# A fused short convolution and leaky-ReLU MLP on one Trainium2 core: the taps' load and softmax, the weight loads and the warm-up matmuls are rearranged

## The chip, the core and the metric

The kernel runs on one core of a Trainium2 chip. A core has five engines with an instruction queue each: TensorE (PE in the profile, its weight loads PEld), VectorE (DVE), ScalarE (ACT), GpSimd (POOL) and SyncE (SP). Data moves between the chip's main memory and the on-chip memory by DMA; a load or store is asked for by an instruction in the queue of SP, ACT or POOL. Engines wait for each other, and for DMAs, by semaphores. The metric is the time of the program on the device in microseconds (us).

## What is computed

The input `x` is 8 x 4096 x 192 (batch, sequence, channels), in float32. The channels form 8 heads of 24; each head has 7 taps.

```python
w = softmax(weight, axis=-1)                  # (8 heads, 7 taps)
# causal convolution along the sequence, the same taps for all 24 channels of a head
out[b, s, h, g] = sum_k w[h, k] * x_pad[b, s + k, h, g]     # 6 zeros ahead of the sequence
h = out.reshape(32768, 192) @ moe_w_in         # (192, 2048)
g = np.maximum(0.01 * h, h)
result = g @ moe_w_out                         # (2048, 192), float32
```

## The kernel before

The 32768 tokens are cut into 32 blocks: a block is 512 positions of two batch rows at a time (index `e`, 0 or 1). Channels are cut into 3 chunks (`c`) of 64, so that 64 channels of row `e = 0` lie on partitions 0 to 63 and the same channels of row `e = 1` on partitions 64 to 127. The stages of a block:

- `load_x` (line 71): two DMAs from SP, one for each `e`, into `x_nat`, float32, tokens on partitions, 384 KB each. Three buffers.
- `cast_x` (line 83): to bfloat16, `x_bf`. In the loop on ScalarE, in halves; for block 0 one half on VectorE and one on ScalarE.
- `transpose_x` (line 96): 24 small matmuls with the identity on TensorE, to PSUM tiles `ptr`; `evac_x` (line 112) copies them to `xt`, channels on partitions.
- `conv_jobs` (lines 128 and 134): for each chunk seven VectorE operations, one multiply and six multiply-adds, with the taps `wk[:, c, k]` as a scalar for each partition. The result is `yt`.
- `mm1` (lines 235 and 242): for each of 16 slices `f` of 128 of the 2048 inner features, six matmuls of 64 rows (three chunks, two `e`, which use the two halves of the array) to the PSUM tile `ph`, and a ScalarE activation (Prelu, alpha 0.01) to `g`.
- `mm2` (line 253): the second product, 128 tokens at a time into `po`, with `w_out` as the moving operand; `evac_o` (line 295) copies `po` to `o_sb` on VectorE, and SP stores it (line 298).

The loop over blocks runs the first product of block `blk` beside the second product of block `blk - 1`; the convolution of block `blk + 1`, and the cast and transposes of block `blk + 2`, are spread over the eight steps of a block. So in the first pass of the loop there is no second product, and `w_out` is used from the second pass on. The order of the instructions on each engine is the order in which the code is written (`manual_schedule`); the tile framework puts in the waits. It hands the DMAs of SP and ACT eight completion semaphores in turn (`DMAHW0` to `DMAHW7` in the rows below), and a DMA that takes one again waits first for the DMA that had it.

Ahead of the loop stands the start, on which the change works. Before: SP loads block 0 of x; the raw taps are loaded straight into `wk`, spread over the partitions by 14 small DMAs with a repeated source, dealt in turn to ACT, POOL and SP (line 163); SP loads block 1, then `moe_w_in` into the float32 tile `w_stage` in eight DMAs (line 172: four quarters of the features, each twice, once for each half of the partitions); POOL loads `w_out` with a cast to bfloat16 (line 177); SP loads block 2. Then block 0 is cast, transposed and copied, the softmax of the taps is done on 128 partitions (lines 192 to 202), block 0 is convolved, block 1 is cast, transposed and copied, and ScalarE casts the four quarters of `w_stage` to `w_in` (line 215). TensorE then runs 56 warm-up matmuls into a tile that nobody reads (line 221), of which each uses 64 rows of the array. They stand in TensorE's queue ahead of the first product.

Of the kernel before, what the change touches and what calls it, by code (L numbers as in the profile page):

```python
# [9 lines left out]
FP32 = mybir.dt.float32  # L10
BF16 = mybir.dt.bfloat16
# [3 lines left out]
def kernel(  # L15
# [8 lines left out]
    nc = tc.nc  # L24

    B, S, D = x.shape
    H, K = weight.shape
    Din, F = moe_w_in.shape
    GRP = D // H
    HALO = 16  # L30
# [4 lines left out]
    CH = 64  # L35
    NCH = D // CH
    ST = 512
    SUB = ST // 128
    NFC = F // 128
# [6 lines left out]
    WQ = 4  # L46

    const_pool = ctx.enter_context(tc.tile_pool(name="const", bufs=1))
# [4 lines left out]
    g_pool = ctx.enter_context(tc.tile_pool(name="g", bufs=3))  # L53
    o_pool = ctx.enter_context(tc.tile_pool(name="o", bufs=4))
    psum_h = ctx.enter_context(tc.tile_pool(name="ph", bufs=2, space=bass.MemoryType.PSUM))
# [7 lines left out]
    x_nat, x_bf, xt, ptr = {}, {}, {}, {}  # L63

    def load_x(blk):
        if blk >= NBLK:
            return
        rp, st = divmod(blk, NB)
        t = stage_pool.tile([128, 2, SUB, D], FP32, name="x_nat")
        for e in range(2):  # L70
            nc.sync.dma_start(  # L71
                out=t[:, e, :, :],
                in_=x[2 * rp + e, st * ST : (st + 1) * ST, :].rearrange(
                    "(c p) d -> p c d", p=128
                ),
            )
        x_nat[blk] = t

    def cast_x(blk, e, copy, half=None):
        if blk not in x_bf:  # L80
            x_bf[blk] = xb_pool.tile([128, SUB, NCH, 2, CH], BF16, name="x_bf")
        s = slice(0, SUB) if half is None else slice(half * SUB // 2, (half + 1) * SUB // 2)
        copy(  # L83
            out=x_bf[blk][:, s, :, e, :],
            in_=x_nat[blk][:, e, s, :].rearrange("p s (c k) -> p s c k", c=NCH),
        )
# [16 lines left out]
    def evac_x(blk, copy):  # L103
        rp, st = divmod(blk, NB)
        if st == 0:
            xt[rp] = xt_pool.tile([128, NCH, HALO + S], BF16, name="xt")
            nc.vector.memset(xt[rp][:, :, 0:HALO], 0.0)
        dst = xt[rp][:, :, HALO + st * ST : HALO + (st + 1) * ST].rearrange(
            "p c (s i k) -> p i s c k", s=SUB, i=2
        )  # L110
        for i, t in enumerate(ptr.pop(blk)):
            copy(out=dst[:, i], in_=t)  # L112
# [4 lines left out]
    def conv_jobs(blk):  # L117
        rp, st = divmod(blk, NB)
        y = yt_pool.tile([128, NCH, ST], BF16, name="yt")
        yt[blk] = y  # L120
        jobs = []
        for c in range(NCH):
            for k in range(K):
                src = xt[rp][:, c, BASE + k + st * ST : BASE + k + (st + 1) * ST]
                dst = y[:, c, :]
                if k == 0:
                    jobs.append(
                        lambda s=src, d=dst, c=c: nc.vector.tensor_scalar_mul(  # L128
                            d, s, wk[:, c, 0:1]
                        )  # L130
                    )
                else:
                    jobs.append(
                        lambda s=src, d=dst, c=c, k=k: nc.vector.scalar_tensor_tensor(  # L134
                            out=d, in0=s, scalar=wk[:, c, k : k + 1], in1=d,
                            op0=mybir.AluOpType.mult, op1=mybir.AluOpType.add,
                        )
                    )
        return jobs


    load_x(0)
    ident = const_pool.tile([128, 128], BF16)
    make_identity(nc, ident)

    wk = const_pool.tile([128, NCH, K], FP32, name="wk")
    parts = []
    for c in range(NCH):
        lo = c * CH
        while lo < (c + 1) * CH:  # L150
            h = lo // GRP
            n = 1
            hi = min((h + 1) * GRP, (c + 1) * CH)
            if lo == h * GRP:
                while (h + n + 1) * GRP <= (c + 1) * CH:
                    n += 1
                    hi = (h + n) * GRP
            parts += [(e * CH + lo - c * CH, c, h, n, (hi - lo) // n) for e in range(2)]
            lo = hi
    queues = [nc.scalar, nc.gpsimd, nc.sync]  # L160
    for i, (p, c, h, n, m) in enumerate(parts):
        src = weight[h : h + n, :]
        queues[i % 3].dma_start(  # L163
            out=wk[p : p + n * m, c, :],
            in_=bass.AP(tensor=src.tensor, offset=src.offset, ap=[[K, n], [0, m], [1, K]]),
        )
    load_x(1)
    w_stage = g_pool.tile([128, NCH, F], FP32, name="w_stage", tag="g")
    for q in range(WQ):
        for e in range(2):  # L170
            fs = slice(q * F // WQ, (q + 1) * F // WQ)
            nc.sync.dma_start(
                out=w_stage[e * CH : (e + 1) * CH, :, fs],
                in_=moe_w_in[:, fs].rearrange("(c p) f -> p c f", p=CH),
            )
    w_out = const_pool.tile([128, NFC, D], BF16)
    nc.gpsimd.dma_start(out=w_out, in_=moe_w_out.rearrange("(c p) d -> p c d", p=128))  # L177
    load_x(2)


    nmax = const_pool.tile([128, NCH], FP32)
    ssum = const_pool.tile([128, NCH], FP32)
    junk = const_pool.tile([128, 1], FP32)
    nc.vector.memset(junk, 0.0)
    nc.scalar.activation(out=junk, in_=junk, func=mybir.ActivationFunctionType.Exp)  # L185

    cast_x(0, 0, nc.vector.tensor_copy)
    cast_x(0, 1, nc.scalar.copy)
    transpose_x(0)
    evac_x(0, nc.vector.tensor_copy)  # L190

    nc.vector.tensor_reduce(  # L192
        out=nmax, in_=wk, axis=mybir.AxisListType.X, op=mybir.AluOpType.max,
    )
    nc.vector.tensor_sub(wk, wk, nmax.unsqueeze(2).to_broadcast((128, NCH, K)))  # L195
    nc.scalar.activation(out=wk, in_=wk, func=mybir.ActivationFunctionType.Exp)  # L196
    nc.vector.tensor_reduce(
        out=ssum, in_=wk, axis=mybir.AxisListType.X, op=mybir.AluOpType.add,
    )
    nc.vector.tensor_scalar_add(ssum, ssum, 1e-9)  # L200
    nc.vector.reciprocal(ssum, ssum)
    nc.vector.tensor_mul(wk, wk, ssum.unsqueeze(2).to_broadcast((128, NCH, K)))

    for job in conv_jobs(0):
        job()

    cast_x(1, 0, nc.scalar.copy)
    cast_x(1, 1, nc.scalar.copy)
# [4 lines left out]
    for q in range(WQ):  # L213
        fs = slice(q * F // WQ, (q + 1) * F // WQ)
        nc.scalar.copy(out=w_in[:, :, fs], in_=w_stage[:, :, fs])  # L215


    wa = psum_h.tile([128, 2, ST], FP32, name="warm", tag="ph")
    NWARM = 56
    for i in range(NWARM):  # L220
        nc.tensor.matmul(  # L221
            out=wa[:, 0, :], lhsT=ident[0:CH, :], rhs=xt[0][0:CH, 0, HALO : HALO + ST],
            start=(i == 0), stop=(i == NWARM - 1),
        )


    g, po, osb, seal = {}, {}, {}, {}
# [75 lines left out]
    for blk in range(NBLK + 1):  # L303
# [3 lines left out]
        for j in range(STEPS):  # L307
            n = (blk - 1) * STEPS + j
# [47 lines left out]
```

## Time and profile before

| | us |
|---|---|
| time, median of 3 runs | 740.72 (740.41 to 740.81) |
| time of the profiled execution | 740.75 |
| its span, first to last instruction | 738.9 |
| TensorE busy, of the span | 712.5 (96%) |
| VectorE busy | 567.0 (77%) |
| ScalarE busy | 555.1 (75%) |
| GpSimd busy | 5.0 (1%) |
| first block of x being cast on VectorE, start | 4.44 |
| first convolution, start | 15.69 |
| warm-up, start | 20.89 |
| first activation `g`, start | 46.29 |

Busy time is a share of the whole span; for a change at the start it tells little. What matters here are the times of single events in the first 70 us. In the profile's rows, L221 is line 221 of the kernel, an arrow `a<-b` means that the instruction writes tile a and reads b, x56 is the number of instructions, and in the timeline the square bracket behind a row tells how long the engine had been idle and who released it. A release is inferred: where an instruction waits for several things, the one that came last by the profile is named. Rows that begin with two numbers have the start and the duration, both in us. A suffix q (SPq, ACTq) means the engine's queue issuing a DMA.

### The profile page before, as it was taken

The page shows a single profiled execution, that of the slowest core. Times are in us where ns is not written, and L with a number is a line of the kernel's source. Part 1 is how long each engine was busy: PE and PEld are TensorE (multiplying, and loading weights), DVE is VectorE, ACT ScalarE, POOL GpSimd, SP SyncE. Part 2 cuts the span into 40 slices and gives each one's busy share as a digit, 9 for nine tenths or more (in the row PEclk, how much of TensorE's full clock was granted, in tenths as well). Part 3 has the DMA queues.
Part 4 walks back from the last instruction along what each step waited for, and adds up shares of the span by engine and source line. Part 5 has one row for each costly group of instructions (what it writes and reads, how often), then busy time and mean ns, then how long its engine had stood idle before and what let it go on. Part 6 is the DMA issues. An engine that isn't in the chain of part 4 may idle for free.

```text
span 738.9 us, 26161 instructions
## 1 busy us (share of the span) xinstructions
PE 712.5 (96%) x11944; PEld 608.2 (82%) x11944; DVE 567.0 (77%) x1002; ACT 555.1 (75%) x644; POOL 5.0 (1%) x12
## 2 busy tenths in 40 slices
PE   0998999999999999999999999999999999999998
PEld 0335788888888888888888888888888888888887
DVE  2944888888888888888888888888888888888812
ACT  1448778887777888877778887777888877778771
POOL 2000000000000000000000000000000000000000
PEclk9999999999999999999999999999999999999999
DMA  8900222122222212222222122222212222211111
GB/s 162 247 19 2 87 77 66 56 87 78 88 77 87 77 45 77 88 77 78 87 77 68 54 88 77 88 76 88 77 48 75 87 78 79 85 34 46 34 45 65
DMA packets 72901, 55.96 MB, mean 76 GB/s; under 512 B 5712, under 2 KB 71254, under 8 KB 72790
## 3 DMA queue, kind: packets, MB, share of 16 engines
q1 hardware_dynamic: 70368, 53.49, 23.9%
q0 software_dynamic: 2224, 0.80, 1.0%
q8 instruction: 93, 1.52, 0.8%
q14 instruction: 18, 0.15, 0.1%
q10 hardware_dynamic: 198, 0.00, 0.0%
HBM read 29.90 MB, written 25.17 MB: 75 GB/s over the span
## 4 chain that ended last, share of the span: by engine, by line
PE 95%; DMA 2%; ACT 2%; ACTq 0%; issue 0%; SPq 0%; DVE 0%
PE po L253 46%; PE ph L235 44%; PE warm L221 3%; ACT g L242 2%; DMA x_nat<-in_x_dram 2%; PE ptr L96 2%; DMA wk<-in_weight_dram 1%; ACT x_bf L83 0%; ACTq L163 0%; SPq L71 0%; SPq L163 0%; DVE o_sb L295 0%
## 5 line engine op out<-in xcount | busy, mean ns | idle before, releaser
L242 ACT ACTIVATE g<-ph 128x1024 bf16<-128x1024 f32 x512 | 496.4, 1021 | 144.1 <-PE ph L235 132.6
L134 DVE SCALAR_TENSOR_TENSOR yt<-xt,wk,yt 128x512 bf16<-128x512 bf16 x576 | 431.2, 749 | 14.0
L253 PEld LDWEIGHTS <-g 64*128 64x128 bf16 (+1 forms) x8048 | 374.9, 94 | 32.4 <-issue 0.2
L253 PE MATMUL po<-w_out,g 64*128 64x192 bf16 (+1 forms) x8048 | 399.2, 243 | 0.0
L235 PE MATMUL ph<-yt,w_in 64*128 64x512 bf16 x3072 | 395.1, 377 | 3.3 <-ACT g L242 2.7
L235 PEld LDWEIGHTS <-w_in 64*128 64x128 bf16 x3072 | 233.3, 94 | 59.6 <-issue 9.5
L295 DVE COPY o_sb<-po 128x192 f32<-128x192 f32 x256 | 91.4, 357 | 106.7 <-PE po L253 103.9
L83 ACT CAST x_bf<-x_nat 128x384 bf16<-128x384 f32 (+1 forms) x123 | 64.1, 521 | 3.7 <-DMA x_nat<-in_x_dram 3.7
L112 DVE COPY xt<-ptr 128x768 bf16<-128x768 bf16 x62 | 31.7, 552 | 37.8 <-PE ptr L96 37.8
L96 PE MATMUL ptr<-ident,x_bf 64*128 64x64 bf16 x768 | 19.2, 193 | 19.4 <-ACT x_bf L83 19.4
L96 PEld LDWEIGHTS <-x_bf 64*128 64x128 bf16 x768 | 17.6, 97 | 19.8 <-ACT x_bf L83 19.6
L128 DVE TENSOR_SCALAR yt<-xt,wk 128x512 bf16<-128x512 bf16 x96 | 33.2, 346 | 0.1
L221 PE MATMUL warm<-xt,ident 64*128 64x512 bf16 x56 | 24.1, 631 | 0.0
L221 PEld LDWEIGHTS <-ident 64*128 64x128 bf16 x56 | 8.2, 147 | 15.0 <-issue 15.0
L215 ACT CAST w_in<-w_stage 128x1536 bf16<-128x1536 f32 x4 | 5.9, 1472 | 6.3 <-DMA w_stage<-in_moe_w_in_dram 6.3
L196 ACT ACTIVATE wk<-wk 128x21 f32<-128x21 f32 x1 | 0.2, 222 | 7.6 <-DVE wk L195 7.6
L185 ACT ACT_TABLE_LOAD x1 | 1.3, 1283 | 4.7 <-issue 4.7
L192 DVE TENSOR_REDUCE nmax<-wk 128x3 f32<-128x21 f32 x1 | 0.2, 174 | 5.3 <-DMA x_nat<-in_x_dram 5.3
L83 DVE CAST x_bf<-x_nat 128x768 bf16<-128x768 f32 x1 | 0.7, 657 | 3.6 <-DMA x_nat<-in_x_dram 3.6
L163 POOL DMA_DIRECT2D wk<-in_weight_dram x5 | 3.1, 651 | 0.3 <-issue 0.3
L112 ACT COPY xt<-ptr 128x768 bf16<-128x768 bf16 x2 | 1.5, 802 | 0.9 <-PE ptr L96 0.9
L177 POOL DMA_DIRECT2D w_out<-in_moe_w_out_dram x1 | 1.2, 1248 | 0.0
(14 smaller groups left out, 2.3 us busy)
## 6 DMA issues: line engine op xcount, KB each, us to landing
x_nat<-in_x_dram SPq DMA_DIRECT2D x64, 384.0 KB, 4.4
out_dram<-o_sb SPq DMA_DIRECT2D x128, 192.0 KB, 1.9
w_stage<-in_moe_w_in_dram SPq DMA_DIRECT2D x8, 384.0 KB, 13.9
w_out<-in_moe_w_out_dram POOLq DMA_DIRECT2D x1, 768.0 KB, 12.6
wk<-in_weight_dram ACTq DMA_DIRECT2D x3, 1.3 KB
wk<-in_weight_dram POOLq DMA_DIRECT2D x3, 1.3 KB, 3.9
wk<-in_weight_dram SPq DMA_DIRECT2D x2, 0.4 KB, 5.8
wk<-in_weight_dram SPq DMA_DIRECT2D x2, 0.2 KB
```

The source lines that it names most:

```text
L83: copy(out=x_bf[blk][:, s, :, e, :], in_=x_nat[blk][:, e, s, :].rearrange("p s (c k) -> p s c k", c=NCH),)
L96: nc.tensor.transpose(out=ts[i][:, s, c, :], in_=x_bf[blk][ps, s, c, :, :].rearrange("p e k -> p (e k)"), identity=ident[ps, ps],)
L112: copy(out=dst[:, i], in_=t)
L128: lambda s=src, d=dst, c=c: nc.vector.tensor_scalar_mul(d, s, wk[:, c, 0:1])
L134: lambda s=src, d=dst, c=c, k=k: nc.vector.scalar_tensor_tensor(out=d, in0=s, scalar=wk[:, c, k : k + 1], in1=d, op0=mybir.AluOpType.mult, ...
L163: queues[i % 3].dma_start(out=wk[p : p + n * m, c, :], in_=bass.AP(tensor=src.tensor, offset=src.offset, ap=[[K, n], [0, m], [1, K]]),)
L215: nc.scalar.copy(out=w_in[:, :, fs], in_=w_stage[:, :, fs])
L221: nc.tensor.matmul(out=wa[:, 0, :], lhsT=ident[0:CH, :], rhs=xt[0][0:CH, 0, HALO : HALO + ST], start=(i == 0), stop=(i == NWARM - 1),)
L235: nc.tensor.matmul(out=ph[:, e, :], lhsT=w_in[ps, c, f * 128 : (f + 1) * 128], rhs=y[ps, c, :], start=(c == 0), stop=(c == NCH - 1),)
L242: return nc.scalar.activation(out=g[blk][:, f, :, :], in_=ph, func=mybir.ActivationFunctionType.Prelu, alpha=0.01,)
L253: ins = nc.tensor.matmul(out=po[m], lhsT=g[b][ps, fc, e, s * 128 : (s + 1) * 128], rhs=w_out[ps, fc, :], start=(rt != 1 and fc == 0), stop ...
L295: nc.vector.tensor_copy(out=o_sb[:, n % 2, :], in_=po.pop(n))
```

## The change

1. Taps. One DMA from ACT loads the 8 x 7 taps into `w8`, with heads on 8 partitions. The softmax runs on those 8 partitions. GpSimd builds a 0/1 mask `sel` (8 x 384) with a memset and two `affine_select`; three float32 matmuls with `sel` as the stationary operand copy each head's taps to the partitions of its channels, into a PSUM tile `wps`, from which VectorE copies them to `wk`. All of this stands ahead of block 0's cast in VectorE's and TensorE's queues.
2. x block 1 is asked for right after block 0, with no tap load between.
3. `w_in`: the DMAs for the lower half of the partitions stay on SP, those for the upper half go to ACT, written behind ACT's cast of block 0 and ahead of its casts of block 1. The convolution of block 0 now stands ahead of these loads in the code.
4. `w_out`: its load stays on POOL, now behind a copy of one element of `w_stage` (`pjunk`), the last element of the lower half's last quarter, so it is asked for once that DMA has landed.
5. Warm-up: 40 matmuls instead of 56, each over all 128 rows of the array instead of 64.

The diff, with the softmax and parts that only move left out:

```diff
     load_x(0)
+    w8 = const_pool.tile([H, K], FP32, name="w8")
+    nc.scalar.dma_start(out=w8, in_=weight)
+    load_x(1)
     ident = const_pool.tile([128, 128], BF16)
     make_identity(nc, ident)
+    sel = const_pool.tile([H, NCH, 2, CH], FP32, name="sel")
+    nc.gpsimd.memset(sel, 1.0)
+    for sign, off in ((1, 0), (-1, GRP - 1)):
+        nc.gpsimd.affine_select(
+            out=sel, in_=sel, compare_op=mybir.AluOpType.is_ge, fill=0.0,
+            base=off, channel_multiplier=-sign * GRP,
+            pattern=[[sign * CH, NCH], [0, 2], [sign, CH]],
+        )
...
+    wps = psum_h.tile([128, 2, ST], FP32, name="wps", tag="ph")
+    for c in range(NCH):
+        nc.tensor.matmul(
+            out=wps[:, 0, c * K : (c + 1) * K],
+            lhsT=sel[:, c, :, :].rearrange("h e k -> h (e k)"),
+            rhs=w8, start=True, stop=True,
+        )
...
-        queues[i % 3].dma_start(
-            out=wk[p : p + n * m, c, :],
-            in_=bass.AP(tensor=src.tensor, offset=src.offset, ap=[[K, n], [0, m], [1, K]]),
-        )
-    load_x(1)
...
-            nc.sync.dma_start(
+            (nc.sync, nc.scalar)[e].dma_start(
                 out=w_stage[e * CH : (e + 1) * CH, :, fs],
                 in_=moe_w_in[:, fs].rearrange("(c p) f -> p c f", p=CH),
             )
-    w_out = const_pool.tile([128, NFC, D], BF16)
-    nc.gpsimd.dma_start(out=w_out, in_=moe_w_out.rearrange("(c p) d -> p c d", p=128))
     load_x(2)
...
+    pjunk = const_pool.tile([1, 1], FP32)
+    nc.gpsimd.tensor_copy(out=pjunk, in_=w_stage[0:1, NCH - 1, F - 1 : F])
+    w_out = const_pool.tile([128, NFC, D], BF16)
+    nc.gpsimd.dma_start(out=w_out, in_=moe_w_out.rearrange("(c p) d -> p c d", p=128))
...
-    NWARM = 56
+    NWARM = 40
     for i in range(NWARM):
         nc.tensor.matmul(
-            out=wa[:, 0, :], lhsT=ident[0:CH, :], rhs=xt[0][0:CH, 0, HALO : HALO + ST],
+            out=wa[:, 0, :], lhsT=ident, rhs=xt[0][:, 0, HALO : HALO + ST],
             start=(i == 0), stop=(i == NWARM - 1),
         )
```

How the instructions stand on the engines. SyncE's queue from the second load of x on, before; each row is a DMA, and the square bracket the semaphores that the instruction waits for:

```order
L71 DMA x_nat<-in_x_dram 128x4x192 x2
L163 DMA wk<-in_weight_dram 16x1x7
L163 DMA wk<-in_weight_dram 8x1x7 [waits DMAHW0_49]
L163 DMA wk<-in_weight_dram 8x1x7 [waits DMAHW1_49]
L163 DMA wk<-in_weight_dram 16x1x7 [waits DMAHW2_49]
L71 DMA x_nat<-in_x_dram 128x4x192 [waits DMAHW3_49]
L71 DMA x_nat<-in_x_dram 128x4x192 [waits DMAHW4_49]
L172 DMA w_stage<-in_moe_w_in_dram 64x3x512 [waits DMAHW5_49]
L172 DMA w_stage<-in_moe_w_in_dram 64x3x512 [waits DMAHW6_49]
```

The same place after:

```order
L71 DMA x_nat<-in_x_dram 128x4x192 x4
L202 DMA w_stage<-in_moe_w_in_dram 64x3x512 x2
L202 DMA w_stage<-in_moe_w_in_dram 64x3x512 [waits DMAHW1_49]
L202 DMA w_stage<-in_moe_w_in_dram 64x3x512 [waits DMAHW3_49]
L71 DMA x_nat<-in_x_dram 128x4x192 [waits DMAHW5_49]
```

The four tap loads and their waits are gone from between blocks 0 and 1 of x, six loads go out without a wait, and four of the w_in loads have left this queue.

ScalarE's queue from the start, after (before, five tap loads stood first, and no w_in load was in it); `w_87` is the tile `w8`:

```order
L144 DMA w_87<-in_weight_dram 8x7
L160 ACT_TABLE_LOAD
L160 ACTIVATE junk<-junk 128x1 [waits DVE_49]
L169 ACTIVATE w_87<-w_87,nmax 8x7 [waits DMAHW0_49,DVE_49]
L83 CAST x_bf<-x_nat 128x12x64 [waits DMAHW2_49]
L202 DMA w_stage<-in_moe_w_in_dram 64x3x512 x3
L202 DMA w_stage<-in_moe_w_in_dram 64x3x512 [waits DMAHW4_49]
L83 CAST x_bf<-x_nat 128x12x64 [waits DMAHW3_49]
L83 CAST x_bf<-x_nat 128x12x64
```

The exponential of the softmax now stands ahead of block 0's cast, and four w_in loads stand ahead of block 1's casts, the last of them with a wait for the second half of block 1 of x (`DMAHW4`).

VectorE's queue from the start, before:

```order
L184 MEMSET junk 128x1
L83 CAST x_bf<-x_nat 128x12x64 [waits DMAHW1_49]
L107 MEMSET xt 128x3x8
L112 COPY xt<-ptr_132 128x4x3x64 [waits PE_49]
L112 COPY xt<-ptr_133 128x4x3x64 [waits PE_49]
L192 TENSOR_REDUCE nmax<-wk 128x3 [waits DMAHW1_49,DMAHW2_49,DMAHW0_49,DMAHW3_49,DMASW4_49,DMAHW5_49,DMASW3_49,DMAHW6_49,DMASW2_49,DMAHW7_49,DMASW1_49,DMASW0_49]
```

And after:

```order
L159 MEMSET junk 128x1
L165 TENSOR_REDUCE nmax<-w_87 8x1 [waits DMAHW0_49]
L172 TENSOR_REDUCE ssum<-w_87 8x1 [waits Activation_49]
L175 TENSOR_SCALAR ssum<-ssum 8x1 [waits DVE_49]
L176 RECIPROCAL ssum<-ssum 8x1 [waits DVE_49]
L177 TENSOR_SCALAR w_87<-w_87,ssum 8x7 [waits DVE_49]
L186 COPY wk<-wps 128x21 [waits PE_49]
L83 CAST x_bf<-x_nat 128x12x64 [waits DMAHW1_49]
L107 MEMSET xt 128x3x8
L112 COPY xt<-ptr_121 128x4x3x64 [waits PE_49]
```

The softmax has moved ahead of block 0's cast, and it waits for one load in place of twelve.

More of the change, by code (lines that the diff above doesn't have):

```diff
@@ L142 @@
     load_x(0)
+    w8 = const_pool.tile([H, K], FP32, name="w8")
+    nc.scalar.dma_start(out=w8, in_=weight)
+    load_x(1)
     ident = const_pool.tile([128, 128], BF16)
     make_identity(nc, ident)
-    wk = const_pool.tile([128, NCH, K], FP32, name="wk")
[L147 to L163, printed above, removed]
-            out=wk[p : p + n * m, c, :],
-            in_=bass.AP(tensor=src.tensor, offset=src.offset, ap=[[K, n], [0, m], [1, K]]),
-        )
-    load_x(1)
+    sel = const_pool.tile([H, NCH, 2, CH], FP32, name="sel")
[6 more added lines that the diff above has]
+        )
@@ new lines @@
+    junk = const_pool.tile([128, 1], FP32)
+    nc.vector.memset(junk, 0.0)
+    nc.scalar.activation(out=junk, in_=junk, func=mybir.ActivationFunctionType.Exp)
+    nmax = const_pool.tile([H, 1], FP32)
+    ssum = const_pool.tile([H, 1], FP32)
+    nc.vector.tensor_reduce(
+        out=nmax, in_=w8, axis=mybir.AxisListType.X,
+        op=mybir.AluOpType.max, negate=True,
+    )
+    nc.scalar.activation(
+        out=w8, in_=w8, func=mybir.ActivationFunctionType.Exp, bias=nmax, scale=1.0,
+    )
@@ new lines @@
+    nc.vector.tensor_reduce(
+        out=ssum, in_=w8, axis=mybir.AxisListType.X, op=mybir.AluOpType.add,
+    )
+    nc.vector.tensor_scalar_add(ssum, ssum, 1e-9)
+    nc.vector.reciprocal(ssum, ssum)
+    nc.vector.tensor_scalar_mul(w8, w8, ssum)
+    wps = psum_h.tile([128, 2, ST], FP32, name="wps", tag="ph")
[4 more added lines that the diff above has]
+            rhs=w8, start=True, stop=True,
+        )
@@ L168 @@
+    wk = const_pool.tile([128, NCH, K], FP32, name="wk")
+    nc.vector.tensor_copy(
+        out=wk, in_=wps[:, 0, 0 : NCH * K].rearrange("p (c k) -> p c k", c=NCH)
+    )
+    cast_x(0, 0, nc.vector.tensor_copy)
+    cast_x(0, 1, nc.scalar.copy)
+    transpose_x(0)
+    evac_x(0, nc.vector.tensor_copy)
+    for job in conv_jobs(0):
+        job()
     w_stage = g_pool.tile([128, NCH, F], FP32, name="w_stage", tag="g")
@@ L175 @@
             )
-    w_out = const_pool.tile([128, NFC, D], BF16)
-    nc.gpsimd.dma_start(out=w_out, in_=moe_w_out.rearrange("(c p) d -> p c d", p=128))
     load_x(2)
[L181 to L205, printed above, removed]
     cast_x(1, 0, nc.scalar.copy)
```

## The prediction

> **What bounds the kernel now.** I read the page first, then the chain of waits over the first 70 us, then the timeline of each engine over the same stretch.
>
> ```profile
> span 738.9 us, 26161 instructions
> PE po L253 46%; PE ph L235 44%; PE warm L221 3%; ACT g L242 2%; DMA x_nat<-in_x_dram 2%; PE ptr L96 2%; DMA wk<-in_weight_dram 1%; ACT x_bf L83 0%; ACTq L163 0%; SPq L71 0%; SPq L163 0%; DVE o_sb L295 0%
> ```
>
> Nine tenths of the span is the steady loop, TensorE work that the diff does not touch. Only the start is changed, so the question is when the first `g` (ScalarE's activation of the first product) begins. The chain over the start:
>
> ```profile
> 2.02 4.16 DMA wk<-in_weight_dram
> ...
> 7.40 11.94 DMA x_nat<-in_x_dram
> ...
> 21.07 23.87 PE warm L221 x56
> 44.94 2.44 PE ph L235 x6
> ```
>
> It runs through the tap loads, the late second block of x, its cast, and then 23.87 us of warm-up. ScalarE had its weights ready long before:
>
> ```profile
> 33.36 1.47 ACT L215 CAST w_in<-w_stage 128x1536 bf16<-128x1536 f32 x1 [2.20 <-DMA w_stage<-in_moe_w_in_dram]
> 46.29 1.02 ACT L242 ACTIVATE g<-ph 128x1024 bf16<-128x1024 f32 x1 [11.46 <-PE warm L221]
> ```
>
> The last weight cast ends at 34.83; the first `g` starts at 46.29, after 11.46 us of waiting for the warm-up. The other input is the first convolution on VectorE:
>
> ```profile
> 4.44 0.66 DVE L83 CAST x_bf<-x_nat 128x768 bf16<-128x768 f32 x1 [3.57 <-DMA x_nat<-in_x_dram]
> 7.86 1.02 DVE L112 COPY xt<-ptr 128x768 bf16<-128x768 bf16 x2 [2.73 <-PE ptr L96]
> 14.16 0.17 DVE L192 TENSOR_REDUCE nmax<-wk 128x3 f32<-128x21 f32 x1 [5.29 <-DMA x_nat<-in_x_dram]
> ...
> 15.47 0.18 DVE L202 TENSOR_TENSOR wk<-wk,ssum 128x21 f32<-128x21 f32 x1
> 15.69 0.35 DVE L128 TENSOR_SCALAR yt<-xt,wk 128x512 bf16<-128x512 bf16 x1
> ...
> 30.65 0.35 DVE L128 TENSOR_SCALAR yt<-xt,wk 128x512 bf16<-128x512 bf16 x1
> ```
>
> The first block's convolution runs from 15.69 to 30.65 (14.96 us, where the second block's begins); it could not start before the softmax at 14.16, which waited for taps. So three things end before the first `g`, at 30.65, 34.83 and about 44.8, and all three move.
>
> **The warm-up.** Its pace, beside pairs of half-array matmuls of the same 512 columns in the loop (a row of the chain), and full-array ones of 192 columns in the tail (copies that follow 16 matmuls each):
>
> ```profile
> 21.00:44.30 23.30, 23.30 (x55) 8.01 (x55) 1.00 0.79 186
> 43.49 0.60 PE L235 MATMUL ph<-yt,w_in 64*128 64x512 bf16 x1
> 67.99 1.29 PE ph L235 x12
> 733.97 0.36 DVE L295 COPY o_sb<-po 128x192 f32<-128x192 f32 x1 [0.96 <-PE po L253]
> 735.28 0.36 DVE L295 COPY o_sb<-po 128x192 f32<-128x192 f32 x1 [0.96 <-PE po L253]
> ```
>
> The columns of the first row are window, length, TensorE and weight-load busy, granted clock, DMA. 23.30 / 55 is 0.424 us a matmul (the chain has 23.87 / 56 = 0.426), while in the loop a pair takes 1.29 / 6 = 0.215. So the warm-up ran at half pace to its end, though the clock column says 1.00, and the loop's first products too: 2.44 us for six steps, to 47.4. Half the array never got the fast pace in 23 us; both halves together (from 43.49, the first product) had it after some 3.9 us. [...]
>
> New: 40 matmuls over all 128 rows. In the tail 16 full-array matmuls of 192 columns take 735.28 - 733.97 = 1.31, or 0.43 ns a column, weight loads hidden: 0.22 us for 512 columns. So 3.9 us at 0.426 (9 matmuls), then 31 x 0.22 = 6.8: 10.7 us instead of 23.9. If the pace stays low it is 40 x 0.426 = 17.0.
>
> **The taps.** Gone: 14 small loads on three queues. Added: one load of 8 x 7, six tiny operations, three selection matmuls, one copy from PSUM, and a `sel` mask on GpSimd.
>
> ```profile
> DMA to landing us min/median/max: 3.3/4.1/7.5
> SPq L163 <- DMA wk<-in_weight_dram: 2.2, 1, 2.2
> 4.65 0.74 SPq L163 DMA_DIRECT2D wk<-in_weight_dram  x1
> 1.01 0.29 POOL masks.py:199 TENSOR_SCALAR_AFFINE_SELECT ident<-ident 128x128 bf16<-128x128 bf16 x1
> L96 PE MATMUL ptr<-ident,x_bf 64*128 64x64 bf16 x768 | 19.2, 193 | 19.4 <-ACT x_bf L83 19.4
> 7.00 0.82 PE L96 MATMUL ptr<-ident,x_bf 64*128 64x64 bf16 x24 [7.00 <-ACT x_bf L83]
> ```
>
> ScalarE's first tap load, issued at 0.74, released SyncE at 4.65, and the new one has its place: landing 4.6 (by the landing row 4.04 at the least, and 6.2 as the load in the chain). From the old softmax's start to the convolution's is 15.69 - 14.16 = 1.53; the new one has one operation less (0.21), so 4.65 + 1.32 = 5.97. The mask: two selects over 384 elements at 0.29 per 128 are 1.74, a memset, and start 1.3: ready by about 3.5, under the load. The three matmuls have no row; between 0.1 (three of 24 transposes in 0.82) and 1.9 (three at the warm-up's 0.63). They stream only 7 columns, so I take three transposes, 0.58; with the copy (0.18) and handovers wk is ready at 6.8. VectorE now does this ahead of its cast of x: 6.8 + 0.66 + 0.05, transposes 0.87, evacuation 1.06: convolution from 9.5 instead of 15.69, and finished at 9.5 + 14.96 = 24.45. Here 1.6 us are lost that the old order did not pay (evacuation ends 9.45, not 8.88, plus the softmax ahead of it), and 6.2 won.
>
> **The weights and the second block of x.** SyncE loses four tap loads, on which x block 1 waited until 6.78, and w_out's traffic goes behind w_in.
>
> ```profile
> 6.78 2.50 SPq L71 DMA_DIRECT2D x_nat<-in_x_dram  x2
> 17.56 0.83 ACT L83 CAST x_bf<-x_nat 128x768 bf16<-128x768 f32 x1 [2.75 <-DMA x_nat<-in_x_dram]
> L163 ACTq DMA_DIRECT2D wk<-in_weight_dram x5: 574/677/1255, 0.7 to 4.0; - x5
> 3.00:4.00 1.00, 0.00 (x0) 0.00 (x0) 0.00 (x0) 0.00 (x0) 1.00 (x2) 1.00 1.10 332
> 15.00:29.00 14.00, 8.75 (x44) 3.46 (x45) 13.29 (x23) 6.11 (x6) 0.00 (x0) 1.00 1.07 228
> w_out<-in_moe_w_out_dram POOLq DMA_DIRECT2D x1, 768.0 KB, 12.6
> ```
>
> Last column is GB/s: x alone 332, the stretch of w_in 228. Behind the first half of block 0 (4.44) come its second half and block 1, 1.18 MB, at 332 3.6 us: block 1 lands near 8.0 instead of 17.5 to 19.4. ScalarE: exp until 5.1, cast of block 0 to 5.9, then four w_in issues that are new on this engine, 4 x 0.65, of which the fourth waits for block 1's second half at 8.0, so 8.65; what queues behind them is block 1's casts, 2 x 0.83, to 10.3, then transposes to 11.2. Warm-up 11.2 to 21.9. w_in is 3.15 MB: from 8.0 at 228 it lands at 21.8, last cast (1.47) to 23.3. I give the second queue no gain in bandwidth.
>
> **Sum.** Ends before the first `g`: warm-up 21.9, casts 23.3, convolution 24.45. The convolution is late last; the product's last matmuls (0.377 each in the row below) and the handovers cost 0.5. First `g` at 24.95, against 46.29: 21.3 us earlier. Behind it nothing new is due:
>
> ```profile
> L235 PE MATMUL ph<-yt,w_in 64*128 64x512 bf16 x3072 | 395.1, 377 | 3.3 <-ACT g L242 2.7
> 52.20 0.50 ACT L83 CAST x_bf<-x_nat 128x384 bf16<-128x384 f32 x1
> 63.89 1.31 PE L253 MATMUL po<-w_out,g 64*128 64x192 bf16 x14
> ```
>
> Block 2's cast comes 5.9 us after the first `g`, now at 30.9, its x behind w_in by some 3.5 us (25). w_out, issued once w_in's last lower half has landed (about 21.5), plus 12.6, is there at 34; its first use is 17.6 us after the first `g`, at 42.6. The second convolution ends at 24.45 + 15.0 = 39.5, before block 1's products at about 42. The loop then runs as before. The profiled execution took 740.75 (738.9 of span, 1.85 around it; the median is 740.72): 740.75 - 21.3 = 719.4.
>
> Its own range: tap load 0.6 earlier and matmuls 0.5 shorter, 718.3; load at 6.2 and matmuls 1.9, 722.3. TensorE idles about 2 us before the last third of y; if the pace drops again that adds at most 1.
>
> **Rivals.**
> - The full-array warm-up stays slow. For it: the clock column shows no change anywhere and 56 matmuls did not help. Against: both halves together did. Then 11.2 + 17.0 = 28.2, three slow pairs 1.28 and handover 0.25: first `g` at 29.7, 724.1. Chance 0.10.
> - w_in is late: the two queues disturb each other, or block 2 of x takes its share. It decides once the last quarter lands after 22.9 (rate under 211). At 180 it lands at 25.5, first `g` (1.47 and 0.6 on) at 27.6: 722.1. Chance 0.08.
> - w_out is late (the other side). [...] Price: landing minus 42.6. [...] Chance 0.03 for late but faster, 0.02 for slower.
> - The start was hidden anyway, no gain: against it stands 11.46 us of plain waiting before the first `g` with nothing else due. 0.01.
>
> **How the numbers follow.** Likeliest: 719.4, chance 0.76. Its bounds reach 718.3 to 722.3 and hold the late w_in too; going to 724.6 takes in the slow warm-up, and 718.0 a little luck. A measurement of this kernel can tell about 0.2% (1.5 us) from no change; all cases but two are faster by more: faster 0.97, same 0.01, slower 0.02.
>
> **What would show it.** First `g` near 25, its wait ended by TensorE's products right behind the convolution; convolution from 9.5; warm-up matmuls 0.43 apart for some nine, then 0.22, all over near 22; x casts of block 1 from 8.65; w_in's last cast over before 24; no wait of an output copy for w_out. I am wrong if the warm-up ends near 28, if ScalarE still waits for w_in at 25, or if the first output products start later than 18 us behind the first `g`.

## The result, and the profile after

The changed kernel takes 719.85 us (median of 4 runs, 718.37 to 721.24) against 740.57 (739.70 to 740.81) for the kernel before: a ratio of 0.9722, 95% interval 0.9699 to 0.9745. The profiled execution took 719.16, with a span of 717.5, and is compared with the 740.75 and 738.9 of before.

The page's span, its chain by lines, and three pieces of that chain (start, duration, what):

```profile
span 717.5 us, 26122 instructions
PE po L260 47%; PE ph L242 45%; DMA w_stage<-in_moe_w_in_dram 2%; ACT g L249 2%; PE ptr L96 1%; DMA x_nat<-in_x_dram 1%; ACT x_bf L83 0%; ACT w_in L216 0%; SPq L71 0%; DVE o_sb L302 0%; ACTq L216 0%
```

```profile
9.57 14.21 DMA w_stage<-in_moe_w_in_dram
...
23.86 1.47 ACT w_in L216
25.33 4.73 ACT g L249 x5
```

The warm-up has left the chain. In its place stands the load of w_in, to 23.78, and the cast of its last quarter. The timeline shows both ways to the first `g`, ScalarE's and VectorE's:

```profile
23.86 1.47 ACT L216 CAST w_in<-w_stage 128x1536 bf16<-128x1536 f32 x1 [1.01 <-DMA w_stage<-in_moe_w_in_dram]
25.24 5.80 ACT L249 ACTIVATE g<-ph 128x1024 bf16<-128x1024 f32 x6
```

```profile
2.22 0.15 DVE L165 TENSOR_REDUCE nmax<-w 8x1 f32<-8x7 f32 x1 [1.26 <-DMA w<-in_weight_dram]
...
5.55 0.18 DVE L186 COPY wk<-wps 128x21 f32<-128x21 f32 x1 [1.60 <-PE wps L180]
...
8.47 0.35 DVE L128 TENSOR_SCALAR yt<-xt,wk 128x512 bf16<-128x512 bf16 x1
...
23.44 0.35 DVE L128 TENSOR_SCALAR yt<-xt,wk 128x512 bf16<-128x512 bf16 x1
```

The convolution of block 0 runs from 8.47 to 23.44 (where block 1's begins), before 15.69 to 30.65. The first `g` starts at 25.24 instead of 46.29, 21.05 earlier, and the span is 21.4 shorter. Behind the first `g` next to nothing has changed: 738.9 - 46.29 = 692.6 us before, 717.5 - 25.24 = 692.3 now. Of the 0.35 between them, 0.22 lies in the first six activations, which took 6.02 before and 5.80 now; before, TensorE still ran its first products at half pace there, until about 47. The rest was not traced.

```profile
46.29 6.02 ACT L242 ACTIVATE g<-ph 128x1024 bf16<-128x1024 f32 x6 [11.46 <-PE warm L221]
```

The warm-up, in two windows (window, length, TensorE busy and matmuls, weight loads, granted clock, DMA share, GB/s), and TensorE's timeline at its two ends and at the first use of w_out:

```profile
13.40:17.50 4.10, 4.08 (x10) 1.51 (x10) 1.00 1.06 294
17.50:23.60 6.10, 6.10 (x29) 2.64 (x27) 1.00 1.10 240
```

```profile
4.10 1.42 PE L180 MATMUL wps<-w,sel 8*128 8x7 f32 x6 [4.10 <-DVE w L177]
...
12.59 0.61 PE L228 MATMUL warm<-xt,ident 128*128 128x512 bf16 x1
...
23.66 1.47 PE L242 MATMUL ph<-yt,w_in 64*128 64x512 bf16 x12
...
42.63 1.31 PE L260 MATMUL po<-w_out,g 64*128 64x192 bf16 x14
```

The first starts at 12.59; the second has no record (the page counts 39 of the 40). From 13.41 on ten matmuls start 0.43 apart, and the pace changes at 17.3, 4.7 us after the first start: a dozen matmuls at half pace in all. The other 28 start 0.216 apart. The second window counts one more, begun ahead of it. The clock column is 1.00 in both windows and does not show this change of pace. The kept trace does: its first record of the granted clock begins at 17.34, with full clock, and the column counts the time ahead of it, for which there is no record, as full too. In the kernel before, that first record begins at 47.08.

TensorE is a third way to the first `g`. The warm-up lasts to 23.66, later than the convolution (23.44), and the first products follow it without a wait for `yt`.

### The profile page after: what moved, and what is told of

The parts are those of the page before. It is cut to its first block, busy times and chain, and to the rows that moved or that the text cites. A ratio compares the mean times of both kernels' runs of the same rounds, so it can differ in the third digit from the quotient of the medians.

```text
span 717.5 us, 26122 instructions
## 1 busy us (share of the span) xinstructions
PE 699.9 (98%) x11933; PEld 606.1 (84%) x11934; DVE 567.0 (79%) x1002; ACT 554.9 (77%) x644; POOL 3.7 (1%) x11
## 3 DMA queue, kind: packets, MB, share of 16 engines
HBM read 29.88 MB, written 25.17 MB: 77 GB/s over the span
## 4 chain that ended last, share of the span: by engine, by line
PE 94%; DMA 3%; ACT 2%; SPq 0%; issue 0%; DVE 0%; ACTq 0%
PE po L260 47%; PE ph L242 45%; DMA w_stage<-in_moe_w_in_dram 2%; ACT g L249 2%; PE ptr L96 1%; DMA x_nat<-in_x_dram 1%; ACT x_bf L83 0%; ACT w_in L216 0%; SPq L71 0%; DVE o_sb L302 0%; ACTq L216 0%
## 5 line engine op out<-in xcount | busy, mean ns | idle before, releaser
L228 PE MATMUL warm<-xt,ident 128*128 128x512 bf16 x39 | 10.9, 445 | 0.2 <-issue 0.2
L228 PEld LDWEIGHTS <-ident 128*128 128x128 bf16 x40 | 4.4, 113 | 6.3 <-issue 3.0
```

The source lines that it names most:

```text
L228: nc.tensor.matmul(out=wa[:, 0, :], lhsT=ident, rhs=xt[0][:, 0, HALO : HALO + ST], start=(i == 0), stop=(i == NWARM - 1),)
```

## The experiments

Times are medians, ratios are to the kernel before, which was timed beside each group: 740.75 (first group: the second look, the VectorE cast, one queue, no warm-up), 740.19 (second group: w_out at once, half-array warm-up, the warm-up alone, the old taps), 740.60 (both off the path, the first version with the convolution on TensorE) and 740.89 (the last run).

**The changed kernel again.**

> The changed kernel once more, for the scatter and a second look at its start. Theory A (the last quarter of w_in, which landed at 23.8 in the first trace, and its cast set the first g): 718.4 to 721.2 as in the first runs, and where this profile's time differs from the first (719.16), its first g differs by as much and is again preceded by the last w_in cast. Rival B (the convolution set it, as the prediction had it): the first g stands some 0.5 us behind the end of the convolution in every trace, and the scatter comes from somewhere later in the loop.

718.71 (718.17 to 719.87), ratio 0.9706 (0.9693 to 0.9719), span 716.5. ScalarE and VectorE of this trace:

```profile
22.86 1.47 ACT L216 CAST w_in<-w_stage 128x1536 bf16<-128x1536 f32 x1 [1.05 <-DMA w_stage<-in_moe_w_in_dram]
24.24 5.81 ACT L249 ACTIVATE g<-ph 128x1024 bf16<-128x1024 f32 x6
```

```profile
18.40 0.64 DVE L128 TENSOR_SCALAR yt<-xt,wk 128x512 bf16<-128x512 bf16 x1
23.68 0.35 DVE L128 TENSOR_SCALAR yt<-xt,wk 128x512 bf16<-128x512 bf16 x1
```

The last quarter landed 1.0 earlier, the first `g` started 1.0 earlier, the span is 1.0 shorter, and the first `g` again stands right behind the last cast, as theory A has it. But the convolution ended at 23.68, 0.56 ahead of the `g`, which B's half a microsecond fits as well: in this execution the two ways end together.

**The last quarter's cast on VectorE.**

```diff
-        nc.scalar.copy(out=w_in[:, :, fs], in_=w_stage[:, :, fs])
+        copy = nc.vector.tensor_copy if q == WQ - 1 else nc.scalar.copy
+        copy(out=w_in[:, :, fs], in_=w_stage[:, :, fs])
-    NWARM = 40
+    NWARM = 32
```

> The cast of the last quarter of w_in goes from ScalarE to VectorE, behind block 0's convolution (it is first read 12 products later); 32 warm-up matmuls instead of 40, so that the warm-up ends at 21.9 and not 23.7. Theory A (w_in's last cast was last): the first g moves from 25.3 to about 24.0 (convolution end 23.44 plus 0.6), 1.2 us faster than the changed kernel (718.6 against its median 719.85), and the scatter of 2.9 us between runs shrinks to about 1, since a landing no longer sets the start. Rival B (the convolution was last): no gain, within 0.3 us of the changed kernel. Rival C (the extra VectorE time, some 1.2 us, makes block 1's convolution late): slower by up to 1.2.

719.01 (718.35 to 719.26): no gain over 718.71 in the same group. VectorE, GpSimd and ScalarE of this trace:

```profile
18.41 1.42 DVE L128 TENSOR_SCALAR yt<-xt,wk 128x512 bf16<-128x512 bf16 x1
24.48 1.22 DVE L217 CAST w_in<-w_stage 128x1536 bf16<-128x1536 f32 x1
```

```profile
18.02 0.51 POOL L221 COPY pjunk<-w_stage 1x1 f32<-1x1 f32 x1 [15.07 <-DMA w_stage<-in_moe_w_in_dram]
18.48 1.26 POOL L223 DMA_DIRECT2D w_out<-in_moe_w_out_dram  x1
```

```profile
25.04 5.81 ACT L250 ACTIVATE g<-ph 128x1024 bf16<-128x1024 f32 x6 [2.85 <-PE ph L243]
```

ScalarE now waits 2.85 us for a product, so the cast is out of the way. But one VectorE multiply took 1.42 us instead of 0.35 and the convolution ended at 24.48. That multiply began at 18.41, inside GpSimd's work, and ended at 19.83, as GpSimd's load of w_out did (19.74). In the second look the same multiply took 0.64 and ended at 19.04, with GpSimd's load from 17.68 to 18.94:

```profile
17.68 1.26 POOL L222 DMA_DIRECT2D w_out<-in_moe_w_out_dram  x1
```

In the first trace it began 0.06 before GpSimd's copy and took 0.35. By the time alone this is rival B. The trace says otherwise: the cast no longer holds up the first `g`, and what it freed was lost to a collision. The next run tests the collision.

**Both off the path.** The VectorE cast, 32 matmuls, and the load of w_out moved back to where the kernel before has it, without `pjunk`.

```diff
+    w_out = const_pool.tile([128, NFC, D], BF16)
+    nc.gpsimd.dma_start(out=w_out, in_=moe_w_out.rearrange("(c p) d -> p c d", p=128))
     load_x(2)
...
-    pjunk = const_pool.tile([1, 1], FP32)
-    nc.gpsimd.tensor_copy(out=pjunk, in_=w_stage[0:1, NCH - 1, F - 1 : F])
```

> Two things are taken off the first g at once: the last quarter of w_in is cast on VectorE behind block 0's convolution (as in the run before), and w_out is asked for at once on GpSimd, so that no GpSimd work falls into the convolution; 32 warm-up matmuls. Theory A (the run with the VectorE cast gained nothing because GpSimd's copy and load held VectorE's multiply at 18.41 for 1.07 us): that multiply takes 0.35, the convolution ends at 23.4, first g at 24.0, profiled span 716.3, median about 718.2, the lowest of all so far by 0.5. Rival B (the multiply is slow for another reason): one multiply again takes 0.6 to 1.4 us and the median is 718.7 to 719.9. Rival C (w_out asked for early delays w_in and block 2 of x): first g at 24.6 or later.

717.88 (717.85 to 718.30), ratio 0.9695 (0.9681 to 0.9708), span 716.1, against the 716.3 expected. VectorE, then ScalarE:

```profile
18.40 0.35 DVE L128 TENSOR_SCALAR yt<-xt,wk 128x512 bf16<-128x512 bf16 x1
...
23.44 1.23 DVE L219 CAST w_in<-w_stage 128x1536 bf16<-128x1536 f32 x1
```

```profile
23.95 5.81 ACT L248 ACTIVATE g<-ph 128x1024 bf16<-128x1024 f32 x6 [1.57 <-PE ph L241]
```

The multiply is back at 0.35, the convolution at 23.44, and the first `g` follows it by 0.51. So in these three traces the multiply lost 0.29 and 1.07 us where GpSimd was first, and nothing where GpSimd's copy and load were not there. Two more runs further down agree, in which a multiply began inside GpSimd's load (no warm-up 0.64, old taps 0.55); in all four the multiply ended 0.08 to 0.10 behind the load. The gain of 0.8 in the median over the second look is below what the intervals can separate. In the traces the first `g` is 0.3 earlier than in the second look and 1.1 earlier than in the run with the VectorE cast alone.

**One queue for w_in.**

```diff
-            (nc.sync, nc.scalar)[e].dma_start(
+            nc.sync.dma_start(
```

> All eight w_in loads on SyncE's queue, as before; the rest as in the changed kernel. Theory A (the transfer rate of w_in, 228 to 240 GB/s, is the limit, whichever queue asks): the last quarter lands within 1 us of 23.8, time within 1 us of 719.85. Rival B (the second queue brings bandwidth): the last quarter lands at 27 or later and the time is 723 or more. Rival C (the loads on ScalarE's queue hold up block 1's casts and crowd block 1's own transfer): block 1 lands near 8 instead of 9.5, warm-up ends 1.5 us earlier, time unchanged or up to 1 us faster.

719.18 (718.45 to 719.53), ratio 0.9707 (0.9694 to 0.9721). ScalarE:

```profile
9.27 0.83 ACT L83 CAST x_bf<-x_nat 128x768 bf16<-128x768 f32 x1 [1.07 <-DMA x_nat<-in_x_dram]
...
23.40 1.47 ACT L216 CAST w_in<-w_stage 128x1536 bf16<-128x1536 f32 x1 [2.08 <-DMA w_stage<-in_moe_w_in_dram]
```

The last quarter lands at 23.4, between the 22.9 and 23.8 of two queues. Theory A: the second queue brings nothing. C holds in part: the warm-up starts at 10.91 with one queue, at 11.72 and 12.59 in the two traces of the changed kernel, which changes nothing in the time. But block 1 did not land near 8: ScalarE waited for its second half until 9.27.

**w_out asked for at once** (that part alone).

> The changed kernel with w_out's load asked for at once on GpSimd, without the wait for w_in. Theory A (the start now hangs on the landing of w_in, and w_out takes its share of the transfer): w_out's 0.8 MB written (1.6 MB read) at 238 GB/s push the last quarter of w_in back by 3.3 to 6.6 us: 723 to 726.5. Rival B (the convolution sets the first g and the transfers have room of 1.5 us): at most 2 us slower, below 722.

719.02 (718.49 to 720.72), ratio 0.9715 (0.9696 to 0.9734). Theory A fell: the last quarter is cast at 23.18 and not later than in the changed kernel. ScalarE, then the load itself among the DMA issues (median time to landing in us at the end), then the DMA queues between 9 and 12 us (packets, MB, share), first of this kernel and then of the kernel before:

```profile
23.18 1.47 ACT L218 CAST w_in<-w_stage 128x1536 bf16<-128x1536 f32 x1 [0.96 <-DMA w_stage<-in_moe_w_in_dram]
```

```profile
w_out<-in_moe_w_out_dram POOLq DMA_DIRECT2D x1, 768.0 KB, 25.7
```

```profile
q1 hardware_dynamic: 254, 0.47, 73.7%
q0 software_dynamic: 344, 0.13, 38.6%
```

```profile
q0 software_dynamic: 1242, 0.48, 135.7%
q1 hardware_dynamic: 94, 0.04, 6.7%
```

Queue q0 is w_out's, q1 SyncE's. Asked for after both blocks of x, w_out trickles in beside them over 25.7 us; its first use is far behind. In the kernel before, w_out was asked for at 4.65 and x block 1 only from 6.78, and w_out took nearly everything between 9 and 12. So the wait that the change puts ahead of w_out was not needed. That asking for x first is what made the difference between these two is the likely reading, but other things differ between the two kernels, and it was not tried alone.

**Half-array warm-up.**

```diff
-            out=wa[:, 0, :], lhsT=ident, rhs=xt[0][:, 0, HALO : HALO + ST],
+            out=wa[:, 0, :], lhsT=ident[0:CH, :], rhs=xt[0][0:CH, 0, HALO : HALO + ST],
```

> The changed kernel with its 40 warm-up matmuls over 64 rows of the array, as before, instead of 128. Theory A (half the array does not bring the fast pace): 0.426 us each to the end, from 12.6 to 29.6, first g at about 31, 5.8 us later than in the changed kernel: 725.5. Rival B (time at work counts, not rows): nine slow ones, the rest 0.22, no difference: 719.9.

725.42 (724.56 to 726.28), ratio 0.9797 (0.9781 to 0.9814). The warm-up's window and ScalarE:

```profile
13.30:29.90 16.60, 16.60 (x40) 5.71 (x40) 1.00 1.14 266
```

```profile
31.69 5.81 ACT L249 ACTIVATE g<-ph 128x1024 bf16<-128x1024 f32 x6 [6.20 <-PE warm L228]
```

The starts are 0.43 us apart to the end, and the first products behind them are slow too: ten take 2.41 from 29.88 on, where twelve take 1.47 behind the warm-up of the changed kernel. The first `g` is at 31.69, 0.7 later than expected; the time is theory A's, to 0.1 us. Only the rows were changed, so in this pair of runs the rows make the difference: 0.43 to the end over 64, 0.216 from 17.3 on over 128.

**The warm-up alone, in the kernel before.**

```diff
-    NWARM = 56
+    NWARM = 40
-            out=wa[:, 0, :], lhsT=ident[0:CH, :], rhs=xt[0][0:CH, 0, HALO : HALO + ST],
+            out=wa[:, 0, :], lhsT=ident, rhs=xt[0][:, 0, HALO : HALO + ST],
```

> The kernel before with the new warm-up alone (40 matmuls over 128 rows). Theory A: the warm-up lasts 10.7 us from 20.9 and ends at 31.6; then the last w_in cast, which ended at 34.83, is last, first g at about 34.9 instead of 46.3, 11.4 us faster: 729.3. Rival B (only the count matters, at half pace): 16 x 0.426 = 6.8 us faster, 733.8. Rival C (the start is hidden): 740.6.

728.42 (728.23 to 729.28), ratio 0.9842 (0.9824 to 0.9859): 11.8 of the 20.7 us from this edit alone. The next bound is the one named:

```profile
32.64 1.47 ACT L215 CAST w_in<-w_stage 128x1536 bf16<-128x1536 f32 x1 [1.63 <-DMA w_stage<-in_moe_w_in_dram]
34.02 5.80 ACT L242 ACTIVATE g<-ph 128x1024 bf16<-128x1024 f32 x6
```

**The old taps in the changed kernel** (the 14 loads and the softmax on 128 partitions, as in the diff's minus lines, behind the loads of both blocks of x).

> The changed kernel with the old taps: 14 small loads on three queues, softmax on 128 partitions behind block 0's evacuation; block 1 of x is still asked for ahead of them. Theory A: the softmax waits for the last tap piece until 13 to 16, the convolution ends at 29 to 32, and ScalarE's exponential holds up its w_in loads and block 1's casts, so that warm-up ends at about 31 too: first g at 30 to 33 instead of 25.3, 725 to 728. Rival B (w_in's landing covers the taps): within 1 us of 719.9.

727.80 (727.71 to 728.16), ratio 0.9830 (0.9816 to 0.9845): theory A. VectorE and ScalarE:

```profile
28.63 0.35 DVE L128 TENSOR_SCALAR yt<-xt,wk 128x512 bf16<-128x512 bf16 x1
```

```profile
12.37 7.47 ACTq L199 DMA_DIRECT2D w_stage<-in_moe_w_in_dram  x4
19.89 1.56 ACT L83 CAST x_bf<-x_nat 128x768 bf16<-128x768 f32 x2 [7.30 <-DMA w_stage<-in_moe_w_in_dram]
...
33.41 5.81 ACT L246 ACTIVATE g<-ph 128x1024 bf16<-128x1024 f32 x6 [2.74 <-PE ph L239]
```

The convolution ends at 28.63, 5.2 us later, but the first `g` is 8.2 late: it waits for TensorE. ScalarE's exponential came only at 12.37. Behind it in the same queue stood the four w_in loads, which were issued from 12.37 to 19.84, with a wait for another w_in load among them, and only then block 1's casts, at 19.89 instead of 10.21. With the casts the transposes and the warm-up moved (22.26 to 32.6). So the taps cost most by what was queued behind them, and a good part of that is the w_in loads' own wait.

**No warm-up** (`NWARM = 1`).

> One warm-up matmul instead of 40. Theory A: TensorE starts the first products at half pace (pairs 0.43 us, a product 1.28 against the 1.02 of an activation) and is fast after some 3.9 us of work, so the start loses three or four times 0.26 us: 0.5 to 1 us slower than the changed kernel, 720.4 to 720.9. Rival B (the pace never rises while TensorE waits for activations): block 0 runs at 1.28 a product to its end, 4 us slower, 723.9. Rival C (warm-up is needless): within 0.3 us.

719.79 (718.97 to 720.63), ratio 0.9717 (0.9704 to 0.9730). That is 1.1 above the second look in the same group, and 0.1 below the first measurement of the changed kernel; the intervals overlap, so the times do not decide between A and C. TensorE and ScalarE:

```profile
23.74 4.07 PE L242 MATMUL ph<-yt,w_in 64*128 64x512 bf16 x20 [4.67 <-DVE yt L134]
```

```profile
24.39 1.02 ACT L249 ACTIVATE g<-ph 128x1024 bf16<-128x1024 f32 x1
25.67 1.02 ACT L249 ACTIVATE g<-ph 128x1024 bf16<-128x1024 f32 x1 [0.26 <-PE ph L242]
26.96 3.87 ACT L249 ACTIVATE g<-ph 128x1024 bf16<-128x1024 f32 x4 [0.27 <-PE ph L242]
```

The trace shows A's mechanism: behind the first `g` ScalarE waits twice, 0.26 and 0.27, and the stretch behind the first `g` is 692.9 instead of 692.3. So the 40 matmuls buy some 0.6 us there. Ahead of it the slow products cost some 0.25 more where the convolution is last: the first `g` stands 0.78 behind the convolution's end (23.61) here, and 0.51 in the run with both off the path. The 56 of the kernel before, which brought no pace, cost over 11.

**A version that beats both.** Since the convolution (15 us of VectorE) and the landing of w_in end together, both were moved: block 0's convolution alone goes to TensorE with diagonal matrices of the taps (rounded to bfloat16 there), and only w_in's first quarter is cast ahead of the first `g`, the others on VectorE inside block 1's convolution. w_out is asked for at once.

```diff
+    def diag(c):
+        for k in range(K):
+            nc.vector.tensor_scalar_mul(dg[:, c, k, :], ident, wk[:, c, k : k + 1])
...
+    def conv_pe(c):
+        o = yp1[:, 0, :] if c == 2 else yp0[:, c, :]
+        for k in range(K):
+            nc.tensor.matmul(
+                out=o, lhsT=dg[:, c, k, :], rhs=xt[0][:, c, BASE + k : BASE + k + ST],
+                start=(k == 0), stop=(k == K - 1),
+            )
+        return o
...
+            if blk == 0 and j in (0, 1, 3):
+                cast_w({0: 1, 1: 2, 3: 3}[j], nc.vector.tensor_copy)
```

> Block 0's convolution alone goes from VectorE to TensorE: 21 matmuls with diagonal matrices of the taps (made on VectorE from the identity), which also serve as the warm-up; ScalarE casts only w_in's first quarter ahead of the first g, VectorE the other three inside block 1's convolution; w_out is asked for at once, block 2's casts one step later. Theory (the first g is bound by the convolution and by w_in's landing, each within 1.5 us of the other, and the loop behind the first g always takes 692.3 us of span): y is ready at about 16.5, the first quarter lands at 15.8 and is cast by 17.4: first g at 17.4, span 709.7, time 711.5; up to 3 us more where a quarter of w_in, block 2 of x or block 1's convolution is late inside block 0. Rival B (block 0 becomes bound by landings instead: x block 2 and the later quarters come no earlier than now): ScalarE waits inside block 0 and the gain is under 3 us, 716 or more.

714.26 (713.12 to 715.33), ratio 0.9644 (0.9631 to 0.9657). The median is inside the time expected, near its end, but the first `g` came at 21.42, not 17.4:

```profile
12.43 3.14 PE L227 MATMUL yp<-xt,dg 128*128 128x512 bf16 x7 [0.78 <-DVE yt L234]
```

```profile
21.42 7.75 ACT L271 ACTIVATE g<-ph 128x1024 bf16<-128x1024 f32 x8 [4.52 <-PE ph L264]
```

TensorE waited for VectorE's copy of the first chunk before it began the second (they share a PSUM tile), and seven matmuls still took 3.14. The pace rose at 17.2, inside the third chunk. The last run only puts both chunks ahead of the copies and leaves out the filler matmuls.

> As the run before (block 0's convolution on TensorE), where TensorE waited 3.0 us in all for copies out of a PSUM tile that it was still to write another part of, and ran all 21 matmuls at half pace; now both first chunks are multiplied before either is copied, and the filler matmuls behind the convolution are left out. Theory: 14 matmuls from 8.5, nine slow and five fast, end at 13.5, transposes to 14.3, the third chunk to 15.9, its copy to 16.6; the first quarter's cast ends at 16.9; first g at 17.3 instead of 21.4, up to 1 us of it given back where block 1's convolution ends after block 1 is due: span 709.5 to 710.5, time 711.2 to 712.3. Rival: the pace does not rise, or x block 2 and the later quarters stop ScalarE inside block 0: 713 or more.

712.87 (712.32 to 714.10), ratio 0.9624 (0.9611 to 0.9637): clear of the changed kernel's 0.9699 to 0.9745. TensorE at the convolution and at the start of block 1, and ScalarE:

```profile
8.92 5.95 PE L227 MATMUL yp<-xt,dg 128*128 128x512 bf16 x14 [1.16 <-DVE xt L112]
14.81 0.52 PE L96 MATMUL ptr<-ident,x_bf 64*128 64x64 bf16 x24
...
35.74 1.04 PE L257 MATMUL ph<-yt,w_in 64*128 64x512 bf16 x8 [0.98 <-DVE yt L134]
```

```profile
18.21 7.75 ACT L264 ACTIVATE g<-ph 128x1024 bf16<-128x1024 f32 x8 [0.96 <-PE ph L257]
```

The first `g` is at 18.21, 0.9 later than expected. The 14 matmuls began 0.4 late, and all of them went at half pace, where nine were expected: they ended at 14.87 instead of 13.5, and the transposes followed without a wait for their input. Here the pace rose only 5.6 us after the first start. 1.0 of the gain is given back at 35.74, where block 1's convolution is late, as was allowed for. The time is 0.6 above the expected range.

## Why the prediction was right, and where it was not

The time was right (719.4 against 719.85, the profiled one 719.16), and so was the frame: the gain is the shift of the first `g`, 21.3 predicted and 21.05 measured, and the stretch behind it stays. That the time is so near is partly luck, as the second step shows. The steps:

- **Warm-up.** Nine matmuls at half pace and 31 at 0.22 were predicted, 10.7 us. A dozen at half pace and 28 at 0.22 were measured, 11.1 us from first start to first product; in the second look it was nine at half pace and 10.5 us. The start was mis-sized by more (12.59 instead of 11.2, since block 1 of x was late), so the warm-up ended at 23.66 and not at 21.9. That the rows count was inferred from the old trace, where 56 matmuls over 64 rows stayed 0.427 apart for 23 us. The half-array run shows it: all 40 stayed 0.43 apart, over 16.6 us.
- **The last end was misnamed.** The prediction has the convolution last at 24.45 and w_in's last cast at 23.3. Measured in the profiled execution: 23.44 and 25.33. Two terms were mis-sized, with opposite signs, and the sum came out 0.3 off by that, which is luck. In the second look the two are 23.68 and 24.33, so near each other that with a small collision a cast moved away alone gained nothing.
- **Taps, too slow by 1.0.** The load was put at 4.6, by the row of a tap load issued at the same time; it landed by 2.22. The three selection matmuls took 1.42 (six records of 0.35, starting 0.21 apart, for the three), against 0.58. wk was ready at 5.73, not 6.8, and what then set the convolution's start was ScalarE's half of block 0's cast (5.67 to 6.50), whose x had only just landed. The landing's lower bound of 4.04 was too high: the row it came from had only loads with a repeated source that ran beside 13 others. Which of the two made them slow is not shown.
- **w_in, too fast by 2.0.** Taken as 3.15 MB at 228 from 8.0. Block 1 of x landed at 9.5 rather than 8.0, and w_in at 23.8. This was the second rival (decides from 22.9), and it happened. Its last cast kept the first `g` back by 1.3 us behind the convolution's own end (23.44 and 0.5); the 0.3 against the prediction is what is left of that after the convolution's 1.0. Of the rival's two reasons, the second queue is ruled out by the run with one queue (23.4). The share that block 2 of x takes was not tested, so why w_in is late stays open. That the second queue gives no bandwidth was right (the last quarter at 23.4 with one, at 22.9 and 23.8 with two).
- **w_out.** Landed at 34.8, against 34 predicted, again by two errors of opposite sign: it was asked for at 18.78 instead of 21.5, and took 16.0 instead of 12.6. It was first used at 42.63, without a wait. The prediction gave 0.05 to a w_out that is late, and no run shows GpSimd held up by a busy VectorE: the load's issue took 1.26 inside the convolution, against 1.25 in the kernel before. What the runs show is GpSimd's load holding VectorE up, by up to 1.07 us.
- The chance of 0.76 lay on a case whose named bound was not the one in the profiled run; the cases of faster, same and slower were right.

By parts: the warm-up is worth 11.8 us in the kernel before, and putting the old taps back costs 8.0 in the changed one. The second queue for w_in and w_out's wait brought nothing. Asking for block 1 of x right behind block 0 was not tried alone.

The scatter of the changed kernel (2.9 us over its first four runs, 1.7 over the five of the second look) is larger than that of the run with both taken off (0.45 over five), which fits a start that hangs on a landing and on a collision. But the kernel before spread over 1.7 us too in that group, so the cause of the scatter stays open.

## What to carry to other kernels

At a kernel's start several ways run side by side to the first unit of the loop: write down the end of each, and expect that an edit gains only down to the next end. Warm-up work is worth its cost only if it does bring the pace, which here the distance between matmuls showed (0.43 and 0.216) and the clock column did not (1.00 at both); 56 half-array matmuls cost 11 us, and 40 full-array ones bought 0.6. Once the ways end within a microsecond of each other, moving one gains next to nothing; two have to move together, and a small collision (here a GpSimd load beside a VectorE multiply, 0.29 and 1.07 us) decides the rest.

## What the runs showed of the hardware that was not expected

- The warm-up's back-to-back matmuls over 64 rows did not leave half pace (0.43 us for 512 columns, over 16.6 us in the half-array run and 23 in the kernel before); over 128 rows they did (0.216), 2.9 to 5.6 us after the first start in the nine traces that have them without a pause. So the number of matmuls at half pace differed from trace to trace: nine in the second look, a dozen in the first trace, all 14 in the last run. The clock column was 1.00 on both sides of the change in the changed kernel, whose trace holds no clock record ahead of 17.34.
- A GpSimd load's issue of 1.26 us held a VectorE multiply that began inside it, or in the copy just ahead of it, until it was over (0.64 and 1.42 instead of 0.35), and did nothing to the multiply-adds around it (0.75 each, as elsewhere).
- A load on GpSimd's queue asked for at 2.9, beside x and w_in on the other two queues (q1 73.7% and q10 7.0% between 9 and 12 us, 45.5% and 42.9% between 12 and 15), took 25.7 us for what took 12.6 in the kernel before and 16.0 in the changed one, without slowing the kernel in a way that the times show (719.02 against 719.85 and 718.71).
